# Lightning attention and a SwiGLU FFN on one Trainium2 core: keys of the second tile scaled in small pieces, its state update and the third tile's transposes moved up

## The chip, the core and the metric

The kernel runs on one core of one Trainium2 chip. The core has five engines that run side by side and wait for each other through semaphores: TensorE (PE, with its weight loads as PEld), VectorE (DVE), ScalarE (ACT), GpSimd (POOL) and SyncE (SP). POOL and SP also issue transfers, which run on the core's 16 DMA engines. The metric is the device time of one execution in microseconds (us); lower is better.

## What is computed

Two stages. The first is linear attention with decay, for 4 batches (B) and 8 heads (H), 768 positions (S) and 64 columns a head (D), in blocks of 64 with a running state for each batch and head:

```python
intra = np.einsum('bhic,bhjc->bhij', qb, kb) * Dmask[None]
intra = np.einsum('bhij,bhjd->bhid', intra, vb)
inter = np.einsum('bhid,bhde->bhie', qb * lam_pow[None], kv_state)
out[:, :, sl] = intra + inter
kb_dec = kb * rev_pow[None]
kv_state = lam_block * kv_state + np.einsum('bhsd,bhse->bhde', kb_dec, vb)
```

Its result, as 3072 tokens of 512 columns (x), goes through the second stage:

```python
g = x @ w_gate
silu = g * (1.0 / (1.0 + np.exp(-g)))
val = x @ w_val
return silu * val @ w_out        # w_gate, w_val: 512 x 1536, w_out: 1536 x 512
```

## The kernel before, in words

**Tiles.** The sequence is cut into six tiles (tt = 0 to 5) of 128 positions of all four batches, so a tile is 512 tokens. For each tile the FFN runs twelve units `ffn_fc` (L412): four gate matmuls into the PSUM tile gp, a Silu on ACT into sil, four value matmuls into vp, and a product on DVE into h_sb (L410). Behind them come four `ffn_out` (L416), of twelve matmuls each, one for each batch; a copy on ACT into osb and a write to memory issued by SP follow each. The output of tile 0 is cut in two halves by columns. PSUM tiles of all kinds take turns in six buffers (L62); one more, spb, is separate.

**Attention inside the FFN.** The order of everything is written out by hand. While the FFN of tile tt runs, the attention of tile tt + 1 is woven in: the loop at L529 makes the list of FFN units, and behind unit i it calls the pieces that stand under i in a table (`first` for tile 0, `second` for tile 1, `pieces` for later ones). Each engine gets its instructions in this order and works them off in it. Tile 0's list has 22 entries: eleven ffn_fc, ffn_g and ffn_v of fc 11 (entries 11 and 12), four ffn_fc of tile 1 for batches 0 and 1 alone (256 columns wide), the first halves of the four ffn_out of tile 0, and a fifth narrow ffn_fc. Tile 1's list has 16: five narrow ffn_fc for batches 2 and 3, seven whole ones, and the second halves of tile 0's ffn_out.

**Pieces of tiles 0 and 1.** These two tiles are worked as one block of 128. `prep_k`, `prep_q` (L227, L234) transpose keys and queries on PE; `front0` (L263) makes the masked scores; `values0` (L284) the output of a batch, which `evac` casts into xt, the FFN's input (on ACT, or on DVE for the last batch). `scale_k` (L298) multiplies the keys by their decay, on ACT, one head at a time for all batches: 128x256 elements. `update0` (L313) makes the state's increment from scaled keys (k_s) and v, 32 matmuls of 64x64 columns for each half p of the batches; it lies in a PSUM tile up. `decay0` (L325) multiplies the state on DVE; `cast_kv` (L329) casts the state to bf16 on ACT, into kvb for tile 1 and into ybuf for tile 2. In the program, these casts of kvb wait for the decay that reads the same PSUM tile.

**Pieces of tiles 2 to 5.** These work in two blocks of 64. `turn` (L240) transposes keys or queries by a DMA that SP issues (into kt and qt). `scale_q` (L245, DVE) and `move_q` (L252, SP: transfers into the other half of zbuf) prepare the queries; `front` and `masks` make the scores; `update` (L336) makes the increment from scaled keys and from v, which lies in ybuf; `update_mid` adds it on DVE, `cast_mid` casts the middle state into ybuf on ACT; `values` (L375) multiplies ybuf by zbuf. `attention` (L475) places these pieces: sq says behind which units queries are scaled and moved, su where the update and its addition stand (the cast one unit later), sf where scores and masks stand, sv where the values stand.

**Queues of transfers.** POOL issues all loads, which cast float32 to bf16 (L89, L93, L198, L202). SP issues output writes, `turn` and `move_q`. Each queue takes its instructions in order. `hold` (L259) is a tiny copy on POOL that reads the last column of qt: POOL issues what follows, in `second` the second half of w_out, v of tile 2 into ybuf (first positions 0 to 63, then 64 to 127) and tile 3, only when the transposed queries have landed. `idle` (L205) puts matmuls on zeros into PE's order.

Of the kernel before, what the change touches and what calls it, by code (L numbers as in the profile page):

```python
# [11 lines left out]
AF = mybir.ActivationFunctionType  # L12
# [9 lines left out]
def kernel(  # L22
# [16 lines left out]
    nc = tc.nc  # L39

    B, H, S, D = q.shape
# [35 lines left out]
    qn, kn = {}, {}  # L77
# [127 lines left out]
    def idle(n, into=None):  # L205

        into = spb[:, 0].rearrange("p n t -> p (n t)") if into is None else into
        for _ in range(n):
            nc.tensor.matmul(into, zeros[:, 0:128], zeros[:, 0:into.shape[1]], start=True, stop=True)  # L209

    kt, qts, qs, ks, kvd, kvn, mid, ups, ssbs = {}, {}, {}, {}, {}, {}, {}, {}, {}
# [7 lines left out]
    def own(d, tt, name, shape, pool=load):  # L219
        if tt not in d:  # L220
            d[tt] = pool.tile(shape, BF16, name=name, tag=name)
        return d[tt]
# [40 lines left out]
    def front0(tt, b):  # L263

        if b % 2 == 0:
            sp = [spb[:, h].rearrange("p n t -> p (n t)").rearrange("p (n t) -> p n t", t=128) for h in range(2)]
        else:
            sp = [psum.tile([128, HP, 128], FP32, name="sp", tag="b") for h in range(2)]
        for hp in range(HP):
            for h, ps in enumerate(HALVES):  # L270
                nc.tensor.matmul(sp[h][:, hp, :], kt[tt][ps, b * HP + hp, :], qts[tt][ps, b * HP + hp, :],
                                 start=True, stop=True)
        ssbs[tt, b] = att.tile([128, 2, HP, 128], BF16, name="ssb", tag="ssb", bufs=4)
        for h in range(2):
            nc.vector.tensor_tensor(out=ssbs[tt, b][:, h], in0=sp[h], in1=mask0[:, h], op=ALU.mult)

    def evac(tt, b, op, eng=None):
        xt = xt_of(tt)[:, :, b * BLK:(b + 1) * BLK]
        if eng is nc.vector:
            nc.vector.tensor_copy(out=xt, in_=op)  # L280
        else:
            nc.scalar.copy(out=xt, in_=op)  # L282

    def values0(tt, bs, wait=0, eng=None):  # L284

        for b in bs:
            op = psum.tile([128, HP, 128], FP32, name="op", tag="b")
            idle(wait, op.rearrange("p n t -> p (n t)"))
            ssb = ssbs.pop((tt, b))
            for hp in range(HP):  # L290
                i = b * HP + hp
                for h, ps in enumerate(HALVES if tt else ()):
                    nc.tensor.matmul(op[ps, hp, :], kvb[:, i, h, :], qts[tt][:, i, :], start=True, stop=False)  # L293
                for h, ps in enumerate(HALVES):
                    nc.tensor.matmul(op[ps, hp, :], vn[tt][:, 2 * i + h, :], ssb[:, h, hp, :], start=(tt == 0), stop=True)  # L295
            evac(tt, b, op, eng)

    def scale_k(tt, h):  # L298

        dst = own(ks, tt, "k_s", [128, B * H, D]).rearrange("p (b h) d -> p b h d", b=B)  # L300
        e = 3 if tt > 1 else 2
        nc.scalar.activation(dst[:, :, h], kn[tt].rearrange("p (b h) d -> p b h d", b=B)[:, :, h], AF.Copy,  # L302
                             scale=pw[:, h, e:e + 1])

    def fp32_kv(name):
# [139 lines left out]
    for b in (2, 3):  # L445
        prep_k(0, b, 5 * (b - 2))
    idle(3)
    front0(0, 2)
    values0(0, (0,), 2)
    front0(0, 3)  # L450
    for b in range(1, B):
        values0(0, (b,), 1 if b < 3 else 0, nc.vector if b == 3 else None)

# [16 lines left out]
    def add(at, i, *piece):  # L472
        at.setdefault(i, []).append(piece)

    def attention(tt, at, sq, su, sf, sv):  # L475

        for p in range(2):
            add(at, sq[p], scale_q, tt, p)
            add(at, sq[p], move_q, tt, p)
            add(at, su[p], update, tt, p, range(1 if tt in (2, NBLK - 1) else 2))  # L480
        for p in range(2):
            add(at, sf[p], front, tt, p)
            add(at, su[p], update_mid, p)
            if 2 < tt < NBLK - 1:
                add(at, su[p], update_end, p)
                add(at, su[p] + 2, cast_kv, tt + 1, p)
            add(at, su[p] + 1, cast_mid, tt, p)
            add(at, sf[p], masks, tt, p)
        for b in range(B):
            add(at, sv, values, tt, b)  # L490

    EARLY = 5
    first = {}
    for h in range(H):
        add(first, h // 2, scale_k, 0, h)
    for i in range(4):
        add(first, 4 + i, half_constants, i // 2, i % 2)
    for p in range(2):
        add(first, 4, update0, 0, p)
        add(first, 5 + p, decay0, 0, p)  # L500
        add(first, 5 + p, cast_kv, 1, p)

    for b in range(2):
        add(first, 7, prep_k, 1, b)
        add(first, 8, prep_q, 1, b)
        add(first, 9, front0, 1, b)
        add(first, 10 + b, values0, 1, (b,))
        add(first, 11 + EARLY, prep_k, 1, 2 + b)
        add(first, 12 + EARLY, prep_q, 1, 2 + b)
        add(first, 13 + EARLY, front0, 1, 2 + b)  # L510
        add(first, 15 + EARLY, values0, 1, (2 + b,), 0, (None, nc.vector)[b])
    second = {}
    add(second, 0, turn, 2, k)
    add(second, 0, turn, 2, q)
    add(second, 0, hold, 2)
    add(second, 0, load_wo, 1)
    add(second, 0, load_v, 2)
    add(second, 0, load_tile, 3)
    for h in range(H):
        add(second, (0, 0, 1, 2, 3, 4, 5, 5)[h], scale_k, 1, h)  # L520
    for h in range(H):
        add(second, (6, 6, 7, 7, 8, 9, 10, 10)[h], scale_k, 2, h)
    for p in range(2):
        add(second, 6, update0, 1, p)
        add(second, 9 + p, decay0, 1, p)
        add(second, 8 + p, cast_kv, 2, p)
    attention(2, second, (7, 8), (11, 11), (8, 10), 14)

    for tt in range(NBLK):  # L529
        units = [(ffn_fc, tt, fc) for fc in range(FC)]  # L530
# [10 lines left out]
        if tt < 2:  # L541
            pieces = (first, second)[tt]
        elif tt + 1 < NBLK:
            for h in range(H):
                add(pieces, h // 2, scale_k, tt + 1, h)
            if tt == 2:
                for p in range(2):
                    add(pieces, 0, update, 2, p, (1,))
                for p in range(2):
                    add(pieces, p, update_end, p)  # L550
                    add(pieces, 4 + 4 * p, cast_kv, 3, p)
                attention(3, pieces, (3, 4), (5, 9), (5, 9), 13)
            else:
                attention(tt + 1, pieces, (1, 2), (4, 8), (4, 8), 12)
            if tt + 2 < NBLK:
                add(pieces, 4 if tt == 2 else 0, hold, tt + 1)
                add(pieces, 4 if tt == 2 else 0, load_tile, tt + 2)
# [41 lines left out]
```

## Time and profile before

| what | before |
|---|---|
| time, median of 3 runs | 231.12 us (231.07 to 231.25) |
| the profiled execution: time, span of its instructions | 231.13 us, 229.4 us |
| PE busy | 220.1 us, 96% of the span |
| DVE, ACT, POOL busy | 113.6, 121.0, 53.3 us |
| granted clock of PE | full in all 40 slices |
| PE busy in 30 to 40, 70 to 80, 80 to 90 us | 8.36, 9.10, 9.51 us of 10 |
| first FFN matmul of tile 0; of tile 1 (narrow); of tile 2 | 16.48, 42.95, 82.45 us |

The span runs from the first to the last instruction of the program; the profiled execution's own time is 1.73 us more. The profile page gives busy times by engine, the span in 40 slices, DMA queues, the chain of work that ended last, and groups of equal instructions. The trace behind it can be asked for waits (who stood idle until whom), for single instructions in order of time, for busy time by stretches, and for the time from a transfer's issue to its landing. A row of the timeline reads: start, length, engine, line, operation, output <- input, count, and in brackets the idle time of the engine before it and what ended that. PE rows overlap a little at their ends, because matmuls are pipelined: four 512-column matmuls start 0.86 us after the four before them, though their row is 1.03 us long. A weight load row (PEld) stands for the half of a matmul that loads the stationary operand.

### The profile page before, as it was taken

How to read it: one execution, taken by the hardware profiler on the slowest of the kernel's cores; microseconds unless marked ns; L12 is line 12 of the kernel's file. 1: busy time of each engine (PE TensorE's matmuls, PEld its weight loads, DVE VectorE, ACT ScalarE, POOL GpSimd, SP SyncE). 2: the span in 40 equal slices, each digit the busy share in tenths (PEclk: the TensorE clock that was granted, in tenths of full speed). 3: DMA queues.
4: the chain of work that ended last, by engine and by line, in shares of the span. 5: the costliest groups of instructions: out<-in, count | busy, mean ns of one | idle time of the engine just before them, and what ended most of it. 6: DMA issues, size and time to landing. Idle time of an engine off the chain costs nothing.

```text
span 229.4 us, 4883 instructions
## 1 busy us (share of the span) xinstructions
PE 220.1 (96%) x1995; PEld 115.5 (50%) x2021; DVE 113.6 (50%) x178; ACT 121.0 (53%) x235; POOL 53.3 (23%) x62
## 2 busy tenths in 40 slices
PE   7999979999999899999999999999999999999994
PEld 2644434788655754444544444544544544444443
DVE  2963449445479527788524878314843322231100
ACT  5847455535877565775845736555443533233222
POOL 7999666000293000730036000000000000000000
PEclk9999999999999999999999999999999999999999
DMA  7999999996799999599949998112210011011022
GB/s 112 149 172 195 187 169 185 158 169 98 160 139 174 184 188 151 123 182 189 161 127 134 199 191 125 49 46 65 75 46 30 18 46 46 3 47 46 34 103 94
DMA packets 109319, 27.33 MB, mean 119 GB/s; under 512 B 96368, under 2 KB 106864, under 8 KB 109296
## 3 DMA queue, kind: packets, MB, share of 16 engines
q0 software_dynamic: 83696, 13.90, 79.4%
q1 hardware_dynamic: 25456, 13.11, 25.0%
q8 instruction: 16, 0.26, 0.5%
q14 instruction: 7, 0.06, 0.1%
q10 hardware_dynamic: 144, 0.00, 0.0%
HBM read 28.32 MB, written 6.29 MB: 151 GB/s over the span
## 4 chain that ended last, share of the span: by engine, by line
PE 85%; DVE 4%; issue 3%; DMA 3%; POOL 2%; ACT 2%; DVEq 0%; ACTq 0%; POOLq 0%
PE vp L407 26%; PE ffn_op L423 26%; PE gp L397 26%; DMA v_nat<-in_v_dram 3%; POOL k_nat L89 1%; PE op L383 1%; PE up L344 1%; PE spb L368 1%; DVE kvd L327 1%; PE op L295 1%; DVE h_sb L410 1%; ACT ybuf L311 1%; DVE zbuf L373 1%; PE op L293 1%; ACT kvb L332 1%
## 5 line engine op out<-in xcount | busy, mean ns | idle before, releaser
L410 DVE TENSOR_TENSOR h_sb<-sil,vp 128x512 bf16<-128x512 bf16 (+1 forms) x77 | 49.9, 652 | 87.1 <-PE vp L407 72.0
L407 PE MATMUL vp<-xt,wv_sb 128*128 128x512 bf16 (+1 forms) x302 | 73.8, 365 | 1.5 <-ACT kvb L332 1.3
L397 PE MATMUL gp<-xt,wg_sb 128*128 128x512 bf16 (+1 forms) x292 | 73.4, 365 | 1.8 <-ACT xt L282 0.4
L423 PE MATMUL ffn_op<-wo_sb,h_sb 128*128 128x512 bf16 (+1 forms) x346 | 65.7, 342 | 0.2
L399 ACT ACTIVATE sil<-gp 128x512 bf16<-128x512 f32 (+1 forms) x77 | 44.0, 571 | 39.3 <-PE gp L397 37.3
L423 PEld LDWEIGHTS <-h_sb 128*128 128x128 bf16 x348 | 33.7, 98 | 28.5
L407 PEld LDWEIGHTS <-wv_sb 128*128 128x128 bf16 x308 | 30.1, 98 | 33.3 <-issue 1.7
L397 PEld LDWEIGHTS <-wg_sb 128*128 128x128 bf16 x308 | 28.6, 98 | 29.9 <-issue 1.6
L426 ACT COPY osb<-ffn_op 128x512 f32<-128x512 f32 (+1 forms) x29 | 14.8, 512 | 52.3 <-PE ffn_op L423 50.1
L302 ACT ACTIVATE k_s<-k_nat,pw 128x256 bf16<-128x256 bf16 x48 | 21.9, 499 | 0.1
L373 DVE TENSOR_TENSOR zbuf<-spb,maskh 64x1024 bf16<-64x1024 f32 x16 | 19.5, 1218 | 0.1
L261 POOL COPY held<-qt 128x2 bf16<-128x2 bf16 x3 | 1.0, 337 | 61.3 <-DMA qt<-q_nat 61.3
L89 POOL DMA_DIRECT2D k_nat<-in_k_dram x10 | 12.8, 1280 | 2.0 <-POOLq L583 0.8
L282 ACT CAST xt<-op 128x512 bf16<-128x512 f32 x18 | 9.7, 589 | 4.8 <-PE op L295 2.9
L311 ACT CAST ybuf<-mid 64x512 bf16<-64x512 f32 x16 | 9.8, 615 | 1.7 <-DVE mid L349 1.4
L89 POOL DMA_DIRECT2D q_nat<-in_q_dram x7 | 10.3, 1465 | 1.4 <-DMA q_nat<-in_q_dram 0.9
L311 ACT CAST ybuf<-kv 64x512 bf16<-64x512 f32 x16 | 9.9, 616 | 0.3
L93 POOL DMA_DIRECT2D ybuf<-in_v_dram x8 | 8.8, 1110 | 2.2 <-issue 2.2
L209 PE MATMUL spb<-zeros 128*128 128x512 bf16 x20 | 7.6, 518 | 1.3 <-DVE warm L136 1.2
L248 DVE TENSOR_TENSOR qs<-qt,qsc 128x1024 bf16<-128x1024 bf16 x8 | 5.5, 685 | 2.7 <-DMA qt<-q_nat 2.7
L198 POOL DMA_DIRECT2D wv_sb<-in_moe_w_val_dram x8 | 6.2, 773 | 1.5 <-DMA wv_sb<-in_moe_w_val_dram 0.9
L198 POOL DMA_DIRECT2D wg_sb<-in_moe_w_gate_dram x8 | 6.3, 786 | 0.6 <-DMA wg_sb<-in_moe_w_gate_dram 0.6
(70 smaller groups left out, 127.4 us busy)
## 6 DMA issues: line engine op xcount, KB each, us to landing
out_dram<-osb SPq DMA_DIRECT2D x19, 256.0 KB, 2.0
k_nat<-in_k_dram POOLq DMA_DIRECT2D x4, 512.0 KB, 10.8
q_nat<-in_q_dram POOLq DMA_DIRECT2D x4, 512.0 KB, 14.4
ybuf<-in_v_dram POOLq DMA_DIRECT2D x8, 256.0 KB, 14.1
zbuf<-qs SPq DMA_DIRECT2D x32, 64.0 KB, 6.0
wo_sb<-in_moe_w_out_dram POOLq DMA_DIRECT2D x2, 768.0 KB, 9.7
out_dram<-osb SPq DMA_DIRECT2D x10, 128.0 KB, 4.0
v_nat<-in_v_dram POOLq DMA_DIRECT2D x4, 256.0 KB, 7.7
```

Of the source, the lines that this page charges most:

```text
L89: nc.gpsimd.dma_start(out=d[tt][:, b0 * H:b1 * H], in_=blk_ap(t, tt, b0, b1))
L198: nc.gpsimd.dma_start(out=t[:, :, f0:f1], in_=w.rearrange("(c p) f -> p c f", p=128)[:, :, f0:f1])
L282: nc.scalar.copy(out=xt, in_=op)
L302: nc.scalar.activation(dst[:, :, h], kn[tt].rearrange("p (b h) d -> p b h d", b=B)[:, :, h], AF.Copy, scale=pw[:, h, e:e + 1])
L311: nc.scalar.copy(out=ybuf[HALVES[1 - c], tt % 2, c, p * NPP:(p + 1) * NPP, h], in_=t[HALVES[h]])
L373: nc.vector.tensor_tensor(out=zbuf[ps, :, c, n], in0=spb[ps], in1=maskh[ps], op=ALU.mult)
L397: nc.tensor.matmul(gp, wg_sb[:, mc, fs], xt_of(tt)[:, mc, ts], start=(mc == 0), stop=(mc == MC - 1))
L399: nc.scalar.activation(sil, gp, AF.Silu)
L407: nc.tensor.matmul(vp, wv_sb[:, mc, fs], xt_of(tt)[:, mc, ts], start=(mc == 0), stop=(mc == MC - 1))
L410: nc.vector.tensor_tensor(out=hs[tt][:, fc, ts], in0=gv.pop((tt, fc)), in1=vp, op=ALU.mult)
L423: nc.tensor.matmul(op, hs[tt][:, fc, b * BLK:(b + 1) * BLK], wo_sb[:, fc, cs], start=(fc == 0), stop=(fc == FC - 1))
L426: nc.scalar.copy(out=osb, in_=op)
```

## The change

Three places. First, batch order at the start: scores of batches 2 and 3 of tile 0 are now made before the values of batch 0, and the values of batch 1 have two idle matmuls ahead of them in place of one. Second, tile 0's table: half_constants stand behind units 5 and 6 (4 to 7 before), both decays directly behind the update at unit 4 (5 and 6 before), the values of tile 1's batch 0 one unit later. The keys of tile 1, until now scaled behind units 0 to 5 of tile 1, are scaled behind units 8 to 20 of tile 0, in pieces of two batches (128x128 elements, sixteen instead of eight), and the two transposes of tile 2 are issued behind unit 18 of tile 0 instead of unit 0 of tile 1, where the hold and the loads stay. Third, tile 1's table: with its keys ready, update0 stands behind unit 1 (6 before), its decays behind 2 and 3 (9 and 10), its casts behind 4 and 6 (8 and 9), and the whole attention of tile 2 up to three units earlier, with its second scores now behind the update; the casts of the middle state stand behind units 9 and 10 (12 before).

```diff
-    def scale_k(tt, h):
+    def scale_k(tt, h, b0=0, b1=B):
-        dst = own(ks, tt, "k_s", [128, B * H, D]).rearrange("p (b h) d -> p b h d", b=B)
+        dst = own(ks, tt, "k_s", [128, B * H, D]).rearrange("p (b h) d -> p b h d", b=B)[:, b0:b1]
         e = 3 if tt > 1 else 2
-        nc.scalar.activation(dst[:, :, h], kn[tt].rearrange("p (b h) d -> p b h d", b=B)[:, :, h], AF.Copy,
+        nc.scalar.activation(dst[:, :, h], kn[tt].rearrange("p (b h) d -> p b h d", b=B)[:, b0:b1, h], AF.Copy,
                              scale=pw[:, h, e:e + 1])
...
-    front0(0, 2)
-    values0(0, (0,), 2)
-    front0(0, 3)
-    for b in range(1, B):
-        values0(0, (b,), 1 if b < 3 else 0, nc.vector if b == 3 else None)
+    for b in (2, 3):
+        front0(0, b)
+    for b in range(B):
+        values0(0, (b,), (2, 2, 1, 0)[b], nc.vector if b == 3 else None)
...
-            add(at, su[p] + 1, cast_mid, tt, p)
+            add(at, su[p] + 1 + (p if tt == 2 else 0), cast_mid, tt, p)
...
     for i in range(4):
-        add(first, 4 + i, half_constants, i // 2, i % 2)
+        add(first, 5 + i // 2, half_constants, i // 2, i % 2)
     for p in range(2):
         add(first, 4, update0, 0, p)
-        add(first, 5 + p, decay0, 0, p)
+        add(first, 4, decay0, 0, p)
         add(first, 5 + p, cast_kv, 1, p)
...
-        add(first, 10 + b, values0, 1, (b,))
+        add(first, 11, values0, 1, (b,))
...
+    for h in range(H):
+        add(first, (8, 8, 9, 9, 13, 14, 15, 16)[h], scale_k, 1, h, 0, 2)
+        add(first, 17 + h // 2, scale_k, 1, h, 2, B)
+    add(first, 18, turn, 2, k)
+    add(first, 18, turn, 2, q)
     second = {}
-    add(second, 0, turn, 2, k)
-    add(second, 0, turn, 2, q)
     add(second, 0, hold, 2)
     add(second, 0, load_wo, 1)
     add(second, 0, load_v, 2)
     add(second, 0, load_tile, 3)
     for h in range(H):
-        add(second, (0, 0, 1, 2, 3, 4, 5, 5)[h], scale_k, 1, h)
-    for h in range(H):
-        add(second, (6, 6, 7, 7, 8, 9, 10, 10)[h], scale_k, 2, h)
+        add(second, (0, 1, 2, 3, 5, 5, 7, 7)[h], scale_k, 2, h)
     for p in range(2):
-        add(second, 6, update0, 1, p)
-        add(second, 9 + p, decay0, 1, p)
-        add(second, 8 + p, cast_kv, 2, p)
-    attention(2, second, (7, 8), (11, 11), (8, 10), 14)
+        add(second, 1, update0, 1, p)
+        add(second, 2 + p, decay0, 1, p)
+        add(second, 4 + 2 * p, cast_kv, 2, p)
+    attention(2, second, (5, 7), (8, 8), (6, 9), 14)
```

## The prediction

> **What bounds the kernel now.** I read the page first: PE is busy 96% of the span, the granted clock is full in all 40 slices, and the chain that ended last is 85% PE. So time can only be won where PE stands still. The view of busy time by stretches of 10 us finds PE below 9.8 in three places: 30 to 40 us (8.36), 70 to 80 (9.10), 80 to 90 (9.51). From 90 us on it is 9.84 or more until the tail, so the change can matter only in tiles 0 and 1. The lists of waits name the first place:
>
> ```profile
> POOL held L261 <- DMA qt<-q_nat: 61.3, 3, 22.8
> ...
> ACT kvb L332 <- DVE kvd L327: 3.8, 2, 2.0
> ...
> PE vp L407 <- ACT kvb L332: 1.3, 1, 1.3
> ```
>
> The copies into kvb wait for the decay on DVE (both read one PSUM buffer), so the state's buffer comes free late, and an FFN matmul that wants it waits 1.3 us. The first line seems to cost nothing: POOL stands at the hold until tile 2's transposed queries are there. It decides this prediction. The timeline around PE's second stop:
>
> ```profile
> 73.47 0.69 PE L344 MATMUL up<-ybuf,k_s 64*64 64x64 bf16 x32
> 74.10 4.10 PE L423 MATMUL ffn_op<-wo_sb,h_sb 128*128 128x256 bf16 x36
> ...
> 78.71 0.86 PE L383 MATMUL op<-zbuf,ybuf 128*64 128x64 bf16 x32 [0.33 <-ACT ybuf L311]
> 80.00 0.41 PE L383 MATMUL op<-zbuf,ybuf 128*64 128x64 bf16 x13 [0.42 <-ACT ybuf L311]
> ...
> 82.45 0.81 PE L397 MATMUL gp<-xt,wg_sb 128*128 128x512 bf16 x2 [0.38 <-ACT xt L282]
> ```
>
> The update at 73.47 comes so late that its state, cast into ybuf, is late for the value matmuls, and these for the next tile. Now the queues, SP's rows of the timeline and then POOL's:
>
> ```profile
> 48.80 5.41 SPq L427 DMA_DIRECT2D out_dram<-osb  x4
> 54.33 3.13 SPq L243 DMA_TRANSPOSE kt<-k_nat  x1
> 57.58 1.58 SPq L243 DMA_TRANSPOSE qt<-q_nat  x1
> ```
>
> ```profile
> 61.44 0.19 POOL L261 COPY held<-qt 128x2 bf16<-128x2 bf16 x1 [22.77 <-DMA qt<-q_nat]
> 62.01 1.01 POOL L202 DMA_DIRECT2D wo_sb<-in_moe_w_out_dram  x1 [0.38 <-issue]
> 63.00 2.18 POOL L93 DMA_DIRECT2D ybuf<-in_v_dram  x2
> ```
>
> By the view of each tile's landings kt lands 5.1 us and qt 3.7 us after issue (59.4, 61.3), the first half of tile 2's v 8.5 us after its issue (71.5). PE reads it at 73.47: 2.0 us to spare.
>
> **Tile 0, part by part.** PE's pitch is 0.86 us for four 512-column matmuls (steps of the chain), 1.73 per FFN unit (vp rows start at 20.79, 22.52, 24.24). From prep_k at 31.02 to the first unit of tile 1 at 42.95 PE takes 11.93 us. Its work there: three units 5.18, gp and vp of fc 11 1.73, transposes 0.9, scores 0.7, values 1.0, some 0.4 of gaps: 9.9. With both decays straight behind the update, DVE does them at 26.1 to 27.4 and the casts end at about 28.7 and 30.4; the matmuls that take those buffers start at 30.15 and 31.5. **The 2.0 us go.** What is then late next has room: weights, k, q and v of this stretch landed at 30.2 to 36.6, at least 0.7 us ahead of their new readers. half_constants slide behind h_sb of units 5 and 6, where DVE idles 1.0 us a unit. The one added idle matmul (0.22 at pitch) and the earlier scores lie ahead of the second v piece, issued 8.41, which lands 6.3 later, at 14.7, and for which PE waits anyway: nothing, and 0.2 if that cover were gone. Values of batch 0, one place later, swap with a gp: nothing; both casts of xt end just before the gp that reads them (0.1 if late).
>
> The small pieces: no row shows an ACT scale of 128 elements. Below, half of a whole one (0.45 at pitch, L302): 16 x 0.22 = 3.6 us, no cost; above, a whole one each, 7.2. The nearest row is L164, a 128x128 activation with a scale per partition: 0.39, 0.33 at pitch; 5.3 us against 3.6 before. ACT is idle 1.1 us of a 512-wide unit (1.73 less a sil of 0.60) and has, behind unit 16, four ffn_outs of 1.31 us with one 0.37 copy each. Nothing on the path; at the upper end a sil is 0.3 us late, which six PSUM buffers cover.
>
> **Tile 1.** update0 moves to its front (0.62 us on PE, wherever it stands), its keys are now ready; decays and casts follow, in 256-wide units where DVE and ACT run at up to 0.9 of the unit's 0.87 us, and any lag ends ahead of what follows. The update of tile 2 moves from unit 11 to unit 8, ahead of three units (5.18) and one front (0.47). Without waits PE would reach it at 73.47 - 5.65 - 2.0 - 0.1 = 65.7. **The change thereby adds a wait**: v's first half must have landed. Behind the waiting matmul stands all of PE, and all else waits for PE. So what happens ahead of it no longer counts; only when v lands does. From the update on the work is 229.4 - 73.47 = 155.9 before; add 5.65; take off what goes at the tile's end. There the first cast of xt starts at 80.38, against some 78.6 when the values (1.13 in tile 2's run, 111.58 to 112.71) run unbroken behind ffn_outs that end at 78.0: **1.8 us go**. So the span is Y + 159.8, Y being v's landing. Y was 71.5; break-even is 69.6.
>
> **When does v land?** Y is 10.0 us behind the hold (61.44 to 71.5), the hold 0.1 behind qt's landing L. So Y = L + 10.1 + c, where c is what tile 2's zbuf moves cost, now issued at about 61.5, beside this load: between 0 and 1.0 (four 64 KB transfers at the 279 to 283 GB/s of 58 to 60 us take 0.9); I take 0.4, since the wo load ahead of v runs at a DMA share of 1.4 where k and q loads reach 2.5.
>
> The transposes: the SP queue now has two output writes ahead, not four, and k of tile 2 lands at 34.85 + 14.1 = 48.9. So kt is issued at 49.0, not 54.3. But q of tile 2 lands only at 36.99 + 15.7 = 52.7, and until about 51 the DMA share is 2.4 (156 to 173 GB/s). Under that load hardware queues hardly move: the output write issued at 48.80 lands after 4.2 us, the one of 52.53 after 1.7. Bounds of L: qt cannot be issued before 52.7, so 52.7 + 3.7 = 56.4; above, the pair of tile 3, issued into running loads at 81.15: kt lands after 10.2, qt 1.9 behind it, so 49.0 + 12.0 = 61.0. The undisturbed pair took 7.0 from kt's issue to qt's landing; counted from where the loads thin out, 51.3, that gives **L = 58.3**, and I take it: the load here ends 3.7 us after kt's issue, that of tile 3 7 us. Y = 58.3 + 10.1 + 0.4 = 68.8, 3.1 us after PE's arrival. The two writes left behind the transposes on SP (b = 2, 3) go out some 4 us late; their osb buffers are wanted next at the tile's end. DVE needs qt at about 60.7, behind h_sb of unit 5; even 61.0 would only shift waiting that stands ahead of v's.
>
> A rule bears on this. The Trainium skill (DMA: Bandwidth & Descriptors, Queues, rings and completion order) has each DMA engine round-robin between the queues it has work for, packet by packet; then kt would take half of the engines from 49.0 on. The 4.2 us above speak against an even share; by the rule the sum is that of the first rival, 229.4.
>
> **The sum**: 68.8 + 159.8 = 228.6, against 229.4. The profiled execution took 231.13, 1.73 more than its span, and the median of the runs is 231.12. Forecast: 228.6 + 1.73, **230.3 us**: of 3.8 us of stops, 3.1 come back as the wait for v.
>
> **Rivals.** (1) Transposes share with the loads: kt is through when they end, they end 1.9 us later (the pair's own spacing), q at 54.6, qt between 1.9 and 3.7 later, 57.4. Span 57.4 + 10.5 + 159.8 = 227.7, time 229.4. For it: the loads are many small packets (96368 of 109319 are under 512 B). Against: the late output write.
> (2) The move does little: the transposes gain only what tile 0 gains, L = 61.3 - 2.0 = 59.3; span 229.6, time 231.3, no change. For it: all transfers ahead are DMA-bound and do not move.
> (3) Slower: the transposes crawl as those of tile 3 did, L = 61.0; Y = 71.5, span 231.3, time 233.0. It decides from L = 59.1 on (c at 0.4). For it: DMA share 2.4 at kt's issue, as at 81 us. Against: the load ends 3 us sooner, and no output write stands between kt and qt.
>
> **Chances.** Forecast 0.35, (1) 0.20, (2) 0.22, (3) 0.23. Two runs of this kernel can be told apart from about 0.2%, 0.46 us: faster 0.55, same 0.22, slower 0.23. Both signs are held: the likeliest case alone is 229.6 to 230.7. The range runs from qt's landing plus c at 57.2 to 60.5: 228.8 to 232.2; the far ends, 228.0 (56.4, c 0) and 233.7 (61.0, c 1.0), are left to 2 in 10.
>
> **What the new profile would show.** Right: no PE wait on kvb near 33; kt issued at 49, qt landed near 58.3; weight loads of the update (L344, k_s) waiting some 3 us for v (ybuf<-in_v_dram) near 66 to 69; no wait on ybuf casts behind it. Wrong: the update runs without a wait (then v was early and time falls to 227.2, 155.9 + 5.65 + 65.7 - 1.8 + 1.73), kt is issued after 50, qt lands past 59.1, or PE stops on sil or h_sb in units 13 to 21, where ACT has the small pieces.

## The result and the profile after

| what | before | after |
|---|---|---|
| median of 6 runs each, on one chip | 231.26 us (231.07 to 231.96) | 234.93 us (233.83 to 235.6) |
| the profiled execution: time, span | 231.13, 229.4 us | 235.6, 233.7 us |
| v's first half of tile 2: issued, landed | 63.0, 71.5 us | 60.8, 71.2 us |
| tile 2's update starts on PE | 73.5 us | 71.2 us |
| FFN outputs at the end of tile 1 start | 74.1 us | 80.2 us |

After to before is 1.0154 (95% interval 1.0125 to 1.0183): **1.5% slower**, where 0.4% faster was forecast. Every time of after is above the range.

The slices of the profile page for PE's busy time and granted clock; each digit is 5.8 us of the changed kernel's span:

```profile
PE   7899999999938999999999999999999999999994
PEclk9999999999995899999999999999999999999999
```

The kernel before had a full clock in every slice. Here the twelfth PE digit is a 3, a stop, and the two clock digits behind it are a 5 and an 8. The waits say for what PE stood:

```profile
PEld L344 <- DMA ybuf<-in_v_dram: 5.3, 1, 5.3
PE up L344 <- DMA ybuf<-in_v_dram: 4.8, 1, 4.8
```

That is the wait that the prediction named, on the matmuls it named, 4.8 us long in place of 3.1. The waits for the casts of kvb are gone. PE's timeline around the stop (start, length, engine, line, operation):

```profile
65.38 1.03 PE L407 MATMUL vp<-xt,wv_sb 128*128 128x512 bf16 x4
71.21 1.06 PE L344 MATMUL up<-ybuf,k_s 64*64 64x64 bf16 x32 [4.81 <-DMA ybuf<-in_v_dram]
72.21 1.89 PE L397 MATMUL gp<-xt,wg_sb 128*128 128x512 bf16 x4
73.89 1.91 PE L407 MATMUL vp<-xt,wv_sb 128*128 128x512 bf16 x4
75.74 0.64 PE L368 MATMUL spb<-qs,kt 64*64 64x64 bf16 x32
76.31 1.46 PE L397 MATMUL gp<-xt,wg_sb 128*128 128x512 bf16 x4
77.61 1.03 PE L407 MATMUL vp<-xt,wv_sb 128*128 128x512 bf16 x4
```

Read the starts: four 512-column matmuls that took 0.86 us ahead of the stop take 1.68 and 1.85 behind it. The table by stretches has the clock in its third column from the right:

```profile
66.00:70.00 4.00, 0.41 (x2) 0.00 (x0) 1.55 (x3) 0.18 (x1) 1.46 (x2) 1.00 1.84 188
70.00:72.00 2.00, 0.79 (x30) 0.79 (x32) 0.11 (x1) 0.00 (x0) 0.50 (x1) 0.59 2.35 168
72.00:74.00 2.00, 2.00 (x17) 0.83 (x12) 1.17 (x2) 0.00 (x0) 0.59 (x1) 0.50 2.08 193
74.00:76.00 2.00, 2.00 (x25) 0.62 (x27) 0.09 (x1) 1.71 (x3) 0.00 (x0) 0.50 2.30 172
76.00:78.00 2.00, 2.00 (x35) 0.95 (x27) 1.99 (x3) 0.13 (x1) 0.00 (x0) 0.70 2.47 158
```

The granted clock was 0.50, from 70.4 to 77.2 us by half-microsecond stretches. PE is 100% busy in 72 to 78 and does little more than half the work: a busy share doesn't show this, the clock column does. Last, SP's queue and the chain of waits that leads into the update:

```profile
50.01 3.98 SPq L243 DMA_TRANSPOSE kt<-k_nat  x1
54.10 2.80 SPq L243 DMA_TRANSPOSE qt<-q_nat  x1
56.95 1.05 SPq L427 DMA_DIRECT2D out_dram<-osb  x2
62.24 7.76 SPq L257 DMA_DIRECT2D zbuf<-qs  x8
```

```profile
54.10 5.03 DMA qt<-q_nat
59.17 0.10 issue
59.27 0.18 POOL held L261
59.45 0.38 issue
59.83 1.00 POOL wo_sb L202
60.83 10.34 DMA ybuf<-in_v_dram
71.21 1.06 PE up L344 x32
```

kt is issued 4.3 us sooner than before and lands 1.8 us sooner (57.6). The last DMA piece takes 10.34 us; the same transfer took 8.5 before.

### The profile page after: what moved, and what is told of

Its sections match the earlier page's. It is cut to its first block, busy times and chain, and to the rows that moved or that the text cites. A ratio compares the mean times of both kernels' runs of the same rounds, so it can differ in the third digit from the quotient of the medians.

```text
span 233.7 us, 4919 instructions
## 1 busy us (share of the span) xinstructions
PE 223.6 (96%) x2022; PEld 115.7 (49%) x2022; DVE 113.2 (48%) x178; ACT 122.5 (52%) x243; POOL 52.8 (23%) x62
## 3 DMA queue, kind: packets, MB, share of 16 engines
HBM read 28.32 MB, written 6.29 MB: 148 GB/s over the span
## 4 chain that ended last, share of the span: by engine, by line
PE 82%; DMA 10%; POOL 5%; issue 1%; ACT 0%; POOLq 0%; ACTq 0%
PE ffn_op L423 27%; PE gp L397 24%; PE vp L407 24%; DMA ybuf<-in_v_dram 4%; DMA wv_sb<-in_moe_w_val_dram 4%; DMA qt<-q_nat 2%; PE up L344 2%; PE op L383 2%; POOL k_nat L89 1%; PE spb L368 1%; POOL v_nat L89 1%; POOL wg_sb L198 1%; POOL wv_sb L198 1%; PE op L293 0%; POOL q_nat L89 0%
## 5 line engine op out<-in xcount | busy, mean ns | idle before, releaser
L397 PE MATMUL gp<-xt,wg_sb 128*128 128x512 bf16 (+1 forms) x308 | 76.3, 371 | 0.1
L407 PE MATMUL vp<-xt,wv_sb 128*128 128x512 bf16 (+1 forms) x308 | 75.7, 369 | 0.3 <-DMA wv_sb<-in_moe_w_val_dram 0.3
L302 ACT ACTIVATE k_s<-k_nat,pw 128x256 bf16<-128x256 bf16 (+1 forms) x56 | 23.9, 470 | 0.1
L344 PE MATMUL up<-ybuf,k_s 64*64 64x64 bf16 x224 | 4.4, 201 | 4.8 <-DMA ybuf<-in_v_dram 4.8
L344 PEld LDWEIGHTS <-k_s 64*64 64x64 bf16 x224 | 3.5, 115 | 8.3 <-DMA ybuf<-in_v_dram 5.3
L349 DVE TENSOR_TENSOR mid<-kvd,up 128x512 f32<-128x512 f32 x8 | 5.4, 680 | 4.3 <-PE up L344 4.3
```

The costliest lines, as they stand in the source:

```text
L344: nc.tensor.matmul(ups[p, c][ps, n, :], ks[tt][HALVES[c], 2 * i + h, :], ybuf[HALVES[c], tt % 2, c, i, h, :], start=True, stop=True)
L397: nc.tensor.matmul(gp, wg_sb[:, mc, fs], xt_of(tt)[:, mc, ts], start=(mc == 0), stop=(mc == MC - 1))
L407: nc.tensor.matmul(vp, wv_sb[:, mc, fs], xt_of(tt)[:, mc, ts], start=(mc == 0), stop=(mc == MC - 1))
```

## The experiments

The theory after the result: all of the loss is the stop for v and the lowered clock behind it. The rivals: the clock falls there for another reason; the loads or the other parts of the change cost time of their own. Every ratio is to the kernel before in the same session, with its 95% interval; unless said otherwise the edit is to the changed kernel.

### Does the stop lower the clock?

```diff
-    def update(tt, p, halves):
+    def update(tt, p, halves, wait=0):
...
+        idle(wait, ups[p, halves[0]].rearrange("p n d -> p (n d)"))
```

The number of idle matmuls, `wait`, is 20 for tile 2 and p = 0, and 0 elsewhere.

> The changed kernel with 20 matmuls on zeros (0.217 us each at pitch, 4.3 us) ahead of tile 2's update, into the PSUM tile that the update then fills; they fill the 4.8 us in which PE stood still. Theory (the stop lowers the clock: the granted clock is 0.50 from 72 to 76 us, behind the stop): v lands when it did, about 71.2, the clock stays at 1.00 and the 2.8 us go by which the update, unit 9, a front and a gp behind the stop took longer than at full pitch: 232.2 us. Rival (the clock falls there for another reason, such as what PE does from 70 us on): the same slow rows, 235.0. Rival (both the wait and the clock are harmless to the end): 235.0 too.

Measured: 232.04 us (231.6 to 232.4, ten executions), ratio 1.0032 (1.0021 to 1.0043).

```profile
65.37 4.48 PE L209 MATMUL up<-zeros 128*128 128x512 bf16 x20
70.46 0.69 PE L345 MATMUL up<-ybuf,k_s 64*64 64x64 bf16 x32 [0.61 <-DMA ybuf<-in_v_dram]
71.08 1.04 PE L398 MATMUL gp<-xt,wg_sb 128*128 128x512 bf16 x4
71.95 1.03 PE L408 MATMUL vp<-xt,wv_sb 128*128 128x512 bf16 x4
72.91 0.45 PE L369 MATMUL spb<-qs,kt 64*64 64x64 bf16 x32
```

PE does more work and the kernel is 2.9 us faster than the changed one: the rows behind the update run at full pitch. v lands at 70.4. In a run below that leaves the stop open (its zbuf transfers stand later in the program) v lands at 70.5, nearly the same, and the span there is 232.2 us against 230.3. So the stop itself lowers the clock. How long a stop does it? Fewer idle matmuls leave a longer one:

> As with the 20 idle matmuls, but 8 of them (1.7 us), so that about 3.2 us of stop are left ahead of tile 2's update (with 20 of them PE was through with the unit before at 65.4 and v landed at 70.4). Theory A (a stop has to last about 3.4 us, the length of the window that the Trainium skill, TensorE: Matmul & The Clock Gate, Part 1, gives for the clock gate, before the clock falls): clock 1.00 behind it, 232.0 us as with 20. Theory B (any stop of some us lowers it): half clock for some 3 to 5 us, 234 us.

> The same with 4 idle matmuls (0.9 us): about 4.1 us of stop are left. Theory A: the stop is longer than 3.4 us, so the clock can fall; with windows that run free of the program it would fall in some executions only, 232.0 in some and 234 in others. Theory B: it falls in all, 234 to 235. Rival (only a stop as long as the changed kernel's 4.8 us does it): 232.0 in all.

> 14 idle matmuls (3.0 us) ahead of tile 2's update, so that about 1.9 us of stop are left. Theory (the clock falls at marks 3.4 us apart, when PE has stood still for a good part of the 3.4 us before; 2.25 us were enough in one profile and 1.3 were not in another): clock 1.00 in nearly all executions, 232.0 us, spread under 1 us. Rival (any stop of about 2 us can lower it): some executions at 233.5 or more with a mean clock of 0.993.

| run | stop in its profile | half clock in its profile | executions with a mean clock of 0.993 or less | time, us |
|---|---|---|---|---|
| 20 idle matmuls | 0.6 us | none | 0 of 10 | 231.6 to 232.4 |
| 14 | 2.0 | none | 5 of 10 | 231.9 to 234.4 |
| 8 | 3.0 | none | 8 of 10 | 232.1 to 235.2 |
| 4 | 4.7 | 3.4 us | 9 of 10 | 231.2 to 235.6 |
| none (the changed kernel) | 4.8 | 6.8 | 6 of 6 | 233.8 to 235.6 |

The last column goes with the one before it: with 14 or 8 idle matmuls no execution with the clock up took over 233.0 us, and none with it down under 233.5. (The mean clock of an execution is 0.998 or more where the clock stayed up.) Theory A (3.4 us are needed) falls, and so does the expectation for 14 that 2 us are nearly free; theory B is the nearer. The length of the stop was seen in the profiled execution only, and v's landing varies from one to the next, so the least stop that lowers the clock stays open; the run with 0.6 us in its profile never showed it.

The run mentioned above, with the zbuf transfers later in the program, shows the fall inside a stop. PE stood still from 65.45 to 70.54 us; the third column from the right is the clock:

```profile
64.42 1.03 PE L407 MATMUL vp<-xt,wv_sb 128*128 128x512 bf16 x4
70.54 1.06 PE L344 MATMUL up<-ybuf,k_s 64*64 64x64 bf16 x32 [5.09 <-DMA ybuf<-in_v_dram]
```

```profile
67.00:67.50 0.50, 0.00 (x0) 0.00 (x0) 0.00 (x0) 0.00 (x0) 0.06 (x1) 1.00 1.74 203
67.50:68.00 0.50, 0.00 (x0) 0.00 (x0) 0.00 (x0) 0.00 (x0) 0.00 (x0) 0.72 2.02 193
68.00:68.50 0.50, 0.00 (x0) 0.00 (x0) 0.00 (x0) 0.00 (x0) 0.00 (x0) 0.50 1.84 215
```

A mean of 0.72 in that half microsecond puts the fall at 67.7, 2.3 us into the stop: 3.4 us without work were not needed. Five profiles have a lowered clock; it lasts 3.4 us in two and 6.8 in three, as if it were decided at marks 3.4 us apart. Of the 3.4 us ahead of the fall PE was idle for 2.3, 2.7, 2.8, 3.4 and 3.4; one mark earlier the run with 4 idle matmuls had been idle for 1.3 us of 3.4 and kept its clock. The clock came back one mark later where PE had been idle for at most 0.1 us in between (two profiles), and two marks later where it had been idle for 0.8 us or more (three). This fits all five and would explain why executions of one kernel differ: it depends on where the marks fall in the stop. It is an estimate from these five and was not tested further.

### What is in the wait for v?

First, v without the wait. One run puts v's first half ahead of w_out's second half, the other puts the update back behind unit 11.

```diff
+    def load_v(tt, cs=(0, 1)):
...
     add(second, 0, hold, 2)
+    add(second, 0, load_v, 2, (0,))
     add(second, 0, load_wo, 1)
-    add(second, 0, load_v, 2)
+    add(second, 0, load_v, 2, (1,))
```

> The changed kernel with the first half of tile 2's v loaded ahead of the second half of wo, its second half behind it. Theory: the mechanism of the change is sound and only v's place in POOL's queue is wrong. The first half, issued at about 59.8, lands about 5 to 6 us later, 65 to 66, PE comes at 66.3 and doesn't stop; 4.8 us of stop and 2.8 us of lowered clock go: span 226.1, time 228.0. Rival (the transfers of zbuf and the loads slow each other whatever the order): v lands at 69 or later, 231 or more. Rival (wo's second half, now 3 us later, stops the FFN outputs near 72.6): 229.

Measured: 228.58 us (228.0 to 230.2), ratio 0.9898 (0.9861 to 0.9935). v lands at 64.0, and the update follows on its unit without a stop:

```profile
65.16 1.03 PE L408 MATMUL vp<-xt,wv_sb 128*128 128x512 bf16 x4
66.11 0.69 PE L345 MATMUL up<-ybuf,k_s 64*64 64x64 bf16 x32
```

```diff
-    attention(2, second, (5, 7), (8, 8), (6, 9), 14)
+    attention(2, second, (5, 7), (11, 11), (6, 9), 14)
```

> The changed kernel with tile 2's update behind unit 11 again, as in the kernel before, all else as changed. Theory (all of the loss is the wait for v and its clock): PE comes to the update at 66.3 + 5.65 = 71.9, v's first half is there at 71.2, no stop, clock 1.00; from the update on the work is the 155.9 us of the kernel before, the casts at the tile's end being late again: span 227.8, time 229.7. Rival (the other parts of the change cost time themselves, or the whole load chain is later): a stop stays at the update or elsewhere, 231 or more.

Measured: 228.53 us (228.2 to 228.9), ratio 0.9877 (0.9854 to 0.99), 1.2 us better than expected: a stop of 0.4 for v, and the values at the tile's end run unbroken; in tile 2 a stop of 1.1 for tile 3's scaled queries stands. So without the wait the rest of the change is a gain, and the wait, with the clock that it lowers, is all of the loss.

Then, why v is so late behind qt: 12.0 us, where it was 10.2 before.

```diff
-            add(at, sq[p], move_q, tt, p)
+            add(at, 9 if tt == 2 else sq[p], move_q, tt, p)
```

> The changed kernel with the eight zbuf transfers of tile 2 issued behind unit 9, so behind v's landing. Theory (they are the 1.9 us by which v came later behind qt's landing than in the kernel before): v lands at 69.3, the stop is 2.9 us, and by that shorter stop the clock may stay at 1.00: 230.3; with the lowered clock 233.1. Rival (the transfers don't touch the load): v lands at 71.2 as before, 235.0.

Measured: 234.6 us, ratio 1.0144 (1.011 to 1.0178). On the transfers the run tells nothing: SP had nothing else in between and issued the transfers as soon as the queries were scaled, at 61.3. A place in the program isn't a time when the engine is idle. The next one makes them wait for their data:

```diff
-    attention(2, second, (5, 7), (8, 8), (6, 9), 14)
+    attention(2, second, (7, 8), (8, 8), (9, 10), 14)
```

> The changed kernel with tile 2's queries scaled behind units 7 and 8 and its scores behind 9 and 10 (5, 7 and 6, 9 in the changed one), update and the rest as changed: the zbuf transfers wait for the scaled queries, so they now start some 4 us later, at about 65.5, when wo has nearly landed. (In the run before that had them later in program order SP still issued them as soon as the queries were scaled, at 61.3, so it moved nothing.) Theory (they slow the load beside them): v lands at 68.9, 1.5 us sooner; stop 3.9 us; 233.0 us if the clock falls, 230.5 if not. Rival (they cost the load nothing): v at 70.4, 234.6 us.

Measured: 233.72 us (233.1 to 234.0), ratio 1.009 (1.0062 to 1.0119). Its chain, and SP's row of the zbuf transfers:

```profile
53.58 5.01 DMA qt<-q_nat
...
59.30 1.00 POOL wo_sb L202
60.30 8.34 DMA ybuf<-in_v_dram
```

```profile
64.95 5.14 SPq L257 DMA_DIRECT2D zbuf<-qs  x8
```

qt lands at 58.6 as in the run with 20 idle matmuls, and v at 68.6, not 70.4, 1.8 us sooner. With 20 idle matmuls four of the 64 KB transfers, 0.26 MB, move between qt's landing and v's; here none of their packets has moved by then. Part of the 1.8 us is gone before one of their packets moves, though. The view of the DMA queues from 63 to 66 us, of the run with 20 idle matmuls and of this one (packets, MB, share):

```profile
DMA packets 856, 0.44 MB, mean 146 GB/s; under 512 B 0, under 2 KB 856, under 8 KB 856
q0 software_dynamic: 856, 0.44, 120.3%
```

```profile
DMA packets 1153, 0.53 MB, mean 177 GB/s; under 512 B 148, under 2 KB 1153, under 8 KB 1153
q0 software_dynamic: 1153, 0.53, 139.8%
```

Only the loads' queue moves data in either, but in the first run, where SP has issued the transfers since 61.4, it moves 0.09 MB less, some 0.5 us at 177 GB/s. What slows it there is open: the edit moves queries and scores with the transfers, so DVE's work differs too (two masks from 62.3 to 64.8 in the first run, none here). So the 1.8 us belong to the group of queries, transfers and scores; that most of it is the transfers' is argued from their bytes, not shown alone. The stop is 3.4 us, the clock fell in all four executions, and the scores now wait 1.0 us for masks, which the expectation had not counted. With the stop filled as well:

> Tile 2's queries and scores later, as in the earlier run of that name, and 15 idle matmuls (3.3 us) in the 3.4 us in which PE stood still there. Theory (the loss is the wait for v plus the lowered clock, and the two add up): v lands at 68.6, clock 1.00, the 1.7 us of slow rows go: 232.0 us (233.7 less 1.7), which still has the 1.0 us stop of the scores for the masks. Rival (the later queries cost something else, which the stop hid): 233 or more.

Measured: 231.85 us (231.6 to 232.1), ratio 1.0017 (1.0008 to 1.0027); clock up in all ten. The wait and the clock add up.

### What did moving the transposes bring?

```diff
-    add(first, 18, turn, 2, k)
-    add(first, 18, turn, 2, q)
     second = {}
+    add(second, 0, turn, 2, k)
+    add(second, 0, turn, 2, q)
```

> The changed kernel with the two transposing transfers of tile 2 behind all four output writes again, as in the kernel before; SP's queue is the only one that differs. Theory (the move gains nothing: with the tile 0 edits alone, kt issued at 52.7 landed at 56.9 and qt at 58.8, and in the changed kernels kt issued at 49.4 takes 7.6 us and lands at 57.1, qt at 58.6 to 58.7): qt lands at 58.8, v at 70.5, the same wait and the same time as the changed kernel, 234.7 us. Rival (as the prediction had it, the move brings the transposes forward): qt lands at 60 or later, v at 72, 236 us.

Measured: 235.0 us (234.9 to 235.6), ratio 1.0153 (1.0135 to 1.0171): the time of the changed kernel. In its profile qt lands at 60.1 and v at 72.1, 0.9 us later than in the profile of after, which is the rival's figure; k and q of tile 2 land within about 0.1 us of after's. So in this pair the move brings qt forward by 0.9 us, and the time shows nothing of it. Other profiles spread: qt lands at 58.5 to 59.1 in the kernels with the move, and at 58.8 (the next run), 59.3 and 60.1 in those without.

### What are the other parts worth?

The kernel before with two edits of the change:

```diff
-        add(first, 4 + i, half_constants, i // 2, i % 2)
+        add(first, 5 + i // 2, half_constants, i // 2, i % 2)
-        add(first, 5 + p, decay0, 0, p)
+        add(first, 4, decay0, 0, p)
```

> The kernel before with two edits of the change alone: the decays of tile 0 straight behind its update, the half-block constants behind units 5 and 6. Theory (2.0 us of stops in tile 0 go and come through to the end, since tile 2's update, 2.0 us sooner at 71.5, still finds v's first half, landed at 71.5): 229.2 us, no wait of a vp for kvb. Rival (v's landing takes it back, or the stops turn up elsewhere): 230.5 to 231.2.

Measured: 229.23 us (229.1 to 229.6), ratio 0.9902 (0.9882 to 0.9922). SP's queue of this run:

```profile
46.77 5.86 SPq L427 DMA_DIRECT2D out_dram<-osb  x4
52.74 2.07 SPq L243 DMA_TRANSPOSE kt<-k_nat  x1
54.94 1.62 SPq L243 DMA_TRANSPOSE qt<-q_nat  x1
```

kt, issued at 52.7, lands at 56.9. In the run with 20 idle matmuls it is issued at 49.4 and lands at 57.1. It had gained nothing by its 3.3 us. In the pair of after and the run above it gained a little: issued at 50.0 and 53.2, kt lands at 57.6 and 58.2.

The changed kernel with tile 2's attention where the kernel before has it:

```diff
-    attention(2, second, (5, 7), (8, 8), (6, 9), 14)
+    attention(2, second, (7, 8), (11, 11), (8, 10), 14)
```

> The changed kernel with tile 2's queries, scores and update all at the units of the kernel before (7 and 8, 8 and 10, 11); what is left of the change is tile 0, the small pieces with the earlier update of tile 1, and the earlier transposes. Theory (the small pieces pay by ending the late casts at the tile's end, 0.8 + 0.4 us of stops in the run with tile 0's edits alone, and the zbuf transfers, being later, leave v to land at 68.6): no stop at the update, none at the tile's end, 228.0 us. Rival (the pieces give nothing by themselves, the late casts come back): 229.2 us, as with tile 0's edits alone.

Measured: **227.72 us** (227.6 to 228.1), ratio 0.9841 (0.9824 to 0.9857), the best of all. PE at the end of tile 1:

```profile
71.53 0.69 PE L344 MATMUL up<-ybuf,k_s 64*64 64x64 bf16 x32
72.16 4.10 PE L423 MATMUL ffn_op<-wo_sb,h_sb 128*128 128x256 bf16 x36
76.19 0.76 PE L383 MATMUL op<-zbuf,ybuf 128*64 128x64 bf16 x35
77.12 0.41 PE L383 MATMUL op<-zbuf,ybuf 128*64 128x64 bf16 x13 [0.17 <-ACT ybuf L311]
```

v landed at 68.7, 2.8 us ahead of the update, and of the stops for late casts 0.17 us is left.

Two runs went on from the one with v's first half ahead of w_out. With the transposes back as well:

> The first half of v ahead of wo, and the transposing transfers behind the four output writes again. Theory (the move is worth nothing): as with v first alone, 228.0 to 228.6 us. Rival (early transposes help once PE no longer waits for v): qt at 60 or later, a stop of a front or of the update, 229.5 or more.

Measured: 229.26 us (228.9 to 231.3), ratio 0.9916 (0.989 to 0.9942), between theory and rival; its profile has 1.4 us of stop for w_out, now behind v's first half in the queue, and 1.7 for tile 3's queries. In one of its ten executions the mean clock was 0.993, and that is its slowest (231.3). With tile 3's first scores behind unit 6 in place of 5:

> The first half of v ahead of wo, and in tile 2 the scores of tile 3's first half one unit later (behind unit 6), where they waited 0.5 us for the scaled queries of tile 3. Theory: that stop goes, 228.0 us, and the spread of the runs with v first (228.0 to 230.2) narrows, as it comes from when tile 3's transposed queries land. Rival: another transfer is late next, 228.6.

Measured: 228.93 us (228.8 to 229.4), ratio 0.9896 (0.9876 to 0.9916): the stop of the scores goes, and one of 1.2 us for w_out stands in its place, as the rival said.

## Why the prediction was wrong, point by point

**Tile 0: right.** Two of its edits alone take 2.2 us off (231.41 to 229.23) where 2.0 were counted, and no matmul waits for kvb.

**The small pieces: right.** They cost nothing on the path: the shortest rows of L302 are 0.39 us, the nearest row's figure, and PE nowhere waits for sil or h_sb in units 13 to 21.

**The tile's end: right.** From the first FFN output to the next tile's first matmul PE takes 6.6 us in after (80.19 to 86.81) and took 8.35 before (74.10 to 82.45): 1.7 us, where 1.8 were expected. By time, all that the run with tile 2's attention put back has beyond tile 0's two edits is worth 1.5 us (229.23 less 227.72). That is the pieces, tile 1's early update, the order at the start and the early transposes together; no run takes them apart.

**PE's arrival at the update: right.** 65.7 was forecast; the unit ahead of it is done at 66.2 in the profile after, at 65.3 to 65.6 with the idle matmuls.

**The landing of qt: near in size, wrong in cause.** 58.3 forecast, 59.1 in after, 58.5 to 58.7 with the idle matmuls. The profile of after stands just past two of the prediction's own signs of being wrong: kt is issued at 50.01 (after 50) and qt lands at 59.13 (past 59.1). k of tile 2, which kt reads, landed at 49.9 there, 1.0 us later than before; why is open. The prediction credited the earlier issue of kt; tile 0's gain, by which SP reaches the transposes sooner, does as much without the move in the run with tile 0's edits alone (58.8). This is rival (2)'s mechanism, "the move does little", with a better number than it was given. Rival (1) had kt through when the loads end; in after q's load landed at 53.7 and kt at 57.6, so its sum fails. Its rule, the even turns between queues of the Trainium skill (DMA: Bandwidth & Descriptors, Queues, rings and completion order), is neither shown nor refuted by that: q's load took 15.7 to 16.7 us from issue to landing in the kernels with early transposes, and 15.7 to 16.3 in those without.

**c, the zbuf moves beside the load: mis-sized.** 0.4 was taken, from 0 to 1.0; it is 1.8 (70.4 against 68.6), and 1.9 in after (12.0 from qt to v, less 10.1). The count of four transfers was right. Their price was not: it took 279 to 283 GB/s, the rate of a stretch without loads, where the loads ran at 146 GB/s; at that rate four transfers would take 1.8 us (an estimate). How much of c is theirs alone stays open, as said above. With it and qt's 0.8 us Y is 71.2 and not 68.8, and the wait 4.8 us and not 3.1. Y is thus past the break-even of 69.6: these two terms alone turn the sign. The run with 20 idle matmuls, which has this wait at full clock, takes 232.0 us: slower than before, at the upper end of the range.

**The step that failed: "from the update on the work is" what it was.** The formula Y + 159.8 took for granted that PE comes out of a stop at the speed at which it went in. It holds where the stop is filled: with v at 70.41 the span of the run with 20 idle matmuls is 230.3, the formula gives 230.2. In after it gives 231.0 and 233.7 was measured; the 2.7 us are the half clock (from the update's start to the first FFN output 8.98 us, against 6.29). No rival had this term, so the range ended 1.6 us below the lowest run. Rival (3) had the sign and nearly v's landing (71.5), but by transposes that crawl, and priced the stop at its length alone: 233.0; that it came nearest in time was luck.

The sum of the errors in the profiled span: 59.13 - 58.3 = 0.8 for qt, 12.0 - 10.5 = 1.5 from qt to v, 2.7 for the clock, together 5.0; 233.7 - 228.6 is 5.1.

The price of the clock could have been bounded beforehand. The Trainium skill (TensorE: Matmul & The Clock Gate, Part 1) says that PE's clock is halved after an idle window of about 3.4 us and comes back after a busy one, with windows that run free of the program; a forecast wait of 3.1 us stands beside that figure. The runs agree with the half, and with the length: the lowered stretches are 3.4 or 6.8 us. They differ in how much idleness it takes: in the run whose zbuf transfers were meant to be later the clock fell at 67.7, 2.3 us into the stop, and in the kernel whose profile has a stop of 2.0 us it fell in half of the executions.

## What to carry to other kernels

Moving work of PE ahead of a transfer doesn't only give the wait back; in these kernels, stops of 2 to 6 us by the profile halved PE's clock in half of the executions or more, for 3.4 or 6.8 us, which cost 1.5 to 2.7 us on top, while the profile's page still shows PE as busy. So price a new wait as its length plus that, and leave the consumer where its data are there (this kernel is 3.7 us faster than before with tile 2's queries, scores and update left in place, 3.7 slower with them moved). Before a transfer is issued earlier, see whether it would then only stand in the loads that run; and count what the earlier work itself issues beside the transfer that decides.

## What the runs showed of the hardware that was not expected

- The lowered clock is 0.50, in stretches of 3.4 us (two profiles) or 6.8 us (three), and begins 2.3 to 4.7 us after PE stops.
- Matmuls on zeros ahead of a waiting matmul save 2.9 us of 235 though they compute nothing.
- Transposes issued some 3 us earlier into running loads landed 0.2 us later in one pair of kernels (57.1 against 56.9) and 0.6 earlier in another (57.6 against 58.2).
- v's load landed 1.8 us later where four 64 KB transfers of SP moved ahead of its end. From 63 to 66 us, before any of their packets moved, the loads ran at 146 GB/s against 177; by the transfers' issue, by DVE's other work in that stretch, or by what else is open.
- Open: why the loads of the first 50 us landed 0.2 to 1.0 us later in the profiles of all changed kernels than in that of before (k of tile 2 at 49.1 to 49.9, 48.9 before).
